# Later w_out loads, one GpSimd square instead of five, and a batch squared from PSUM, in a relu² attention and MLP kernel

## The chip, the cores and the metric

The kernel runs on one core of one Trainium2 chip. The metric is the device time of one execution in microseconds (us). Each kernel is built, checked against the reference and run several times; the number quoted is the median. All runs quoted here are in the fast state. A ratio is the mean time of one kernel's fast runs over that of the other's fast runs of the same rounds, so it is not quite the ratio of the medians quoted beside it.

## The reference, cut to what matters

```python
# q, k, v: (8, 12, 448, 64)
scores = np.matmul(q, k.transpose(0, 1, 3, 2)) / np.sqrt(64)
attn   = np.maximum(scores, 0.0) ** 2 / 448
x      = np.matmul(attn, v)            # -> 3584 tokens x 768
h      = x @ w_in                      # 768 x 2048
g      = np.maximum(h, 0.0) ** 2
out    = g @ w_out                     # 2048 x 768
```

There is no softmax: a score tile needs relu, a square and a scale on its way from PSUM to SBUF. Input and output are float32; the kernel computes in float16.

## The kernel before

A batch has three units of four heads. A unit has seven score tiles, numbered t = 0 to 6; a "round" makes one score tile, and round r is unit r // 7, tile r % 7. The opening stage (rounds 0 to 22) makes batch 0 while the weights stream in. After it TensorE works through a fixed mix of later score tiles (`sp`), attention times v (`avt`), x times w_in (`hps`) and g times w_out (`ops`). Program order on TensorE is fixed.

A score tile can be squared in two ways:

```python
def relu2(ps, dst, scale):                       # "from PSUM"
    nc.scalar.activation(out=dst, in_=ps, func=AF.Square, scale=scale)
    nc.vector.scalar_tensor_tensor(              # reads PSUM and one SBUF tile
        out=dst, in0=ps, scalar=0.0, in1=dst, op0=ALU.is_gt, op1=ALU.mult)

def relu2_wide(ps, dst, scale, eng):             # "through SBUF"
    r = rel_p.tile([P, 2, S], FP32, name="rel", tag="wide")
    nc.scalar.activation(out=r, in_=ps, func=AF.Relu, scale=scale)
    eng.tensor_mul(dst, r, r)                    # both inputs are SBUF

def soft(n, t, sp):
    at = at_p.tile([P, 2, S], FP16, name="at", tag="at")
    if n < NPE and t % 2 == 1:                   # NPE = 6, NU = 3
        relu2_wide(sp[:, :, 0:S], at, SK, nc.gpsimd if n and t == 3 else nc.vector)
    else:
        relu2(sp[:, :, 0:S], at, SK)
    ats[n, t] = at
```

So in units 0 to 5 the odd tiles go through SBUF, and tile 3 of units 1 to 5 is squared on GpSimd. GpSimd also casts q and k and issues every load that casts on the way (v, w_in, w_out). In the opening stage its order follows this table:

```python
beside = {                                       # round: what is issued beside it
    ...                                          # cut: w_in parts, transposes, casts
    8: [(turn_pe, 2, "q", act), (load_v, 1, 0)],
    9: [(cast_qk, 3, "k", pool), (cast_qk, 3, "q", pool), ...],
    10: [(load_v, 1, 1)],
    12: [(load_v, 1, 2), (load_w2, 0)],
    13: [(load_w2, 1)],
    ...
    17: [(load_w2, 2)],
    18: [(load_w2, 3)],
    16: [(cast_qk, 4, "k", pool), (cast_qk, 4, "q", pool), ...],
}
for r in range(STREAM):                          # 23 rounds, cut
    sp = scores(n, t)
    soft(n, t, sp)
    for z in late.get(r, (r - LAG,) if LAG <= r else ()):   # LAG = 3
        av(*divmod(z, TJ))
    for fn, *a in beside.get(r, ()):
        fn(*a)
```

Of the kernel before, what the change touches and what calls it, by code (L numbers as in the profile page):

```python
# [16 lines left out]
def kernel(  # L17
# [9 lines left out]
    nc = tc.nc  # L27

    B, H, S, D = q.shape
# [8 lines left out]
    NU = 3  # L38
# [5 lines left out]
    SK = 256.0  # L44
# [29 lines left out]
    def load_qk(n, w, eng):  # L74
        b, u = divmod(n, NU)
        t = raw_p.tile([P, 2, TJ * D], FP32, name=w + "f", tag=w + "f")
        src = q if w == "q" else k
        eng.dma_start(  # L78
            out=t,
            in_=src[b, 4 * u:4 * u + 4].rearrange(  # L80
                "(f e) (p t) d -> (e p) f (t d)", e=2, t=TJ))
        raw[n, w] = t

    def cast_qk(n, w, op):
        src = raw.pop((n, w))
        t = blk_p.tile([P, TJ, 2 * D], FP16, name=w + "s", tag=w + "s")
        op(t.rearrange("p t (f d) -> p f t d", f=2),  # L87
           src.rearrange("p f (t d) -> p f t d", d=D))
        blk[n, w] = t
# [7 lines left out]
    def turn_pe(n, w, op):  # L97
        src = blk.pop((n, w))
        ps = mm_p.tile([P, TJ * P], FP16, name="tps", tag="mm")
        for t in range(TJ):  # L100
            nc.tensor.transpose(ps[:, t * P:(t + 1) * P], src[:, t, :], ident)  # L101
        t = qkt_p.tile([P, TJ, P], FP16, name=w + "T", tag=w + "T")
        op(t.rearrange("p t c -> p (t c)"), ps)
        qkt[n, w] = t

    def load_v(b, us):

        if b not in vst:
            vst[b] = v_p.tile([P, NU, 2, TJ * D], FP16, name="vs", tag="vs")
        src = v[b].rearrange("(u x) (p t) d -> p u x (t d)", x=4, t=TJ)  # L110
        for r in range(2):
            rows = slice(64 * r, 64 * r + 64)
            hs = slice(1, 3) if r else slice(0, 4, 3)
            if isinstance(us, int):
                nc.gpsimd.dma_start(out=vst[b][rows, us], in_=src[:, us, hs])
            else:
                for i, h in enumerate(range(4)[hs]):
                    nc.gpsimd.dma_start(out=vst[b][rows, :, i], in_=src[:, :, h])
# [4 lines left out]
    def load_w1(i):  # L123
        nc.gpsimd.dma_start(
            out=w1[i],
            in_=moe_w_in[:, 512 * i:512 * (i + 1)].rearrange("(m p) f -> p m f", p=P))
# [26 lines left out]
    def relu2(ps, dst, scale):  # L153
        nc.scalar.activation(out=dst, in_=ps, func=AF.Square, scale=scale)  # L154
        nc.vector.scalar_tensor_tensor(  # L155
            out=dst, in0=ps, scalar=0.0, in1=dst, op0=ALU.is_gt, op1=ALU.mult)

    def relu2_wide(ps, dst, scale, eng):

        r = rel_p.tile([P, 2, S], FP32, name="rel", tag="wide")  # L160
        nc.scalar.activation(out=r, in_=ps, func=AF.Relu, scale=scale)
        eng.tensor_mul(dst, r, r)  # L162
# [82 lines left out]
    def scores(n, t):  # L245
        qT, kT = qkt[n, "q"], qkt[n, "k"]
        sp = s_p.tile([P, 2, 512], FP32, name="sp", tag="s")
        for e in range(2):
            for f in range(2):
                c = f ^ e  # L250
                r = slice(64 * f, 64 * f + 64)
                nc.tensor.matmul(  # L252
                    sp[64 * c:64 * c + 64, e, 0:S].rearrange("p (t c) -> p t c", t=TJ),
                    lhsT=kT[r, t, 64 * e:64 * e + 64],
                    rhs=qT[r, :, 64 * e:64 * e + 64], start=True, stop=True)
        return sp

    def soft(n, t, sp):
        at = at_p.tile([P, 2, S], FP16, name="at", tag="at")
        if n < NPE and t % 2 == 1:  # L260
            relu2_wide(sp[:, :, 0:S], at, SK, nc.gpsimd if n and t == 3 else nc.vector)
        else:
            relu2(sp[:, :, 0:S], at, SK)
        ats[n, t] = at
# [3 lines left out]
    def av(n, t):  # L268

        b, u = divmod(n, NU)  # L270
        if n == NU * b and t == 0:
            xts[b] = x_p.tile([P, NM, S], FP16, name="xt", tag="xt")
        vs = vst[b]
        if t == 0:
            avs_open[n] = [mm_p.tile([P, 512], FP32, name="avt", tag="mm") for _ in range(2)]
        ap = avs_open[n]
        at = ats.pop((n, t))
        for e in range(2):
            for c in range(2):
                f = c ^ e  # L280
                r = slice(64 * c, 64 * c + 64)
                nc.tensor.matmul(  # L282
                    ap[f][64 * e:64 * e + 64, 0:S],
                    lhsT=vs[r, u, e ^ c, t * D:(t + 1) * D],
                    rhs=at[r, e, :],
                    start=(t == 0), stop=(t == TJ - 1), skip_group_check=True)
        if t < TJ - 1:
            return
        for f in range(2):
            nc.scalar.activation(  # L290
                out=xts[b][:, 2 * u + f, :], in_=ap[f][:, 0:S], func=AF.Copy, scale=CX)

    pool, dve, act = nc.gpsimd.tensor_copy, nc.vector.tensor_copy, nc.scalar.copy
# [3 lines left out]
    NPE = 6  # L297
# [32 lines left out]
    with tc.manual_schedule():  # L330
        load_qk(0, "k", nc.sync)
        load_qk(0, "q", nc.scalar)
        for n in (1, 2):
            load_qk(n, "k", nc.sync)
            load_qk(n, "q", nc.sync)
        idle = const_p.tile([P, 512], FP16, name="idle", tag="idle")
        nc.vector.memset(idle, 0.0)
        ident = const_p.tile([P, P], FP16, name="ident", tag="ident")
        make_identity(nc, ident)
        for u in range(NU):  # L340
            load_v(0, u)

        warm = mm_p.tile([P, 512], FP32, name="warm", tag="mm")
        for _ in range(12):
            nc.tensor.matmul(warm, lhsT=idle[:, 0:P], rhs=idle, start=True, stop=True)
        cast_qk(0, "k", dve)
        cast_qk(0, "q", act)
        turn_pe(0, "k", dve)
        turn_pe(0, "q", dve)
        for w in "kq":  # L350
            cast_qk(1, w, pool)
        load_w1(0)

        beside = {
            1: [(load_w1, 1)],
            2: [(cast_qk, 2, "k", pool), (cast_qk, 2, "q", pool),
                (load_qk, 3, "k", nc.sync), (load_qk, 3, "q", nc.sync)],
            3: [(turn_pe, 1, "k", dve), (load_w1, 2)],
            5: [(turn_pe, 1, "q", act), (load_w1, 3)],
            7: [(turn_pe, 2, "k", dve)],  # L360
            8: [(turn_pe, 2, "q", act), (load_v, 1, 0)],
            9: [(cast_qk, 3, "k", pool), (cast_qk, 3, "q", pool),
                (load_qk, 4, "k", nc.sync), (load_qk, 4, "q", nc.sync)],
            10: [(load_v, 1, 1)],
            12: [(load_v, 1, 2), (load_w2, 0)],
            13: [(load_w2, 1)],
            14: [(turn_pe, 3, "k", dve)],
            15: [(turn_pe, 3, "q", act)],
            17: [(load_w2, 2)],
            18: [(load_w2, 3)],  # L370
            16: [(cast_qk, 4, "k", pool), (cast_qk, 4, "q", pool),
                 (load_qk, 5, "k", nc.sync), (load_qk, 5, "q", nc.sync)],
        }
        late = {21: (18, 19), 22: (20,)}
        for r in range(STREAM):
            n, t = divmod(r, TJ)
            sp = scores(n, t)
            soft(n, t, sp)
            for z in late.get(r, (r - LAG,) if LAG <= r else ()):
# [3 lines that stand above are left out]
# [3 lines left out]
    for i in range(STREAM // 2, NB):  # L386
        g = []
        for r in range(max(STREAM, 2 * i), 2 * i + 2):
            n, t = divmod(r, TJ)
            g.append((n, t, scores(n, t)))  # L390
        if i in avs:
            for t in range(TJ):
                av(avs[i], t)
        for a in g:
            soft(*a)
        if i in pushes:
            push_dense(pushes[i])
        upkeep(i)
        nxt = min([j for j in pushes if j > i] or [NB + 2])
        run_some(max(0.0, (queued - KEEP) / (nxt - i)))  # L400
# [37 lines left out]
```

## Time and profile before

The time before was 423.14 us (423.02 to 423.86, 3 runs).

| part of the execution | what TensorE does | read in |
|---|---|---|
| 0 to 34 us | opening stage, partly busy | 40-slice row |
| 34.0 to 45.0 us | idle | timeline |
| 52.75 us (sixth slice) to the end | busy 9 tenths or more, but for the last slice (5) | 40-slice row |

The page: the span, TensorE's busy time (us, share, instructions), TensorE's busy tenths in 40 slices of 10.55 us, and the clock granted to TensorE in tenths of full speed.

```profile
span 422.0 us, 7567 instructions
PE 394.7 (94%) x3104; PEld 200.4 (47%) x3104; DVE 248.9 (59%) x300; ACT 260.0 (62%) x407; POOL 80.9 (19%) x101
PE   6771699999999999999999999999999999999995
PEclk9866599999999999999999999999999999999999
```

The fourth slice is a hole in a kernel that is otherwise full. The list of waits for 30 to 50 us (who waited for whom: us in total, times, longest) names the cause and what stood before it:

```profile
PE avt L282 <- POOL at L162: 11.0, 1, 11.0
POOL vs L115 <- DMA w_1_91<-in_moe_w_in_dram: 5.7, 1, 5.7
POOL w_0_94 L129 <- DMA w_2_92<-in_moe_w_in_dram: 4.8, 1, 4.8
POOL w_1_95 L129 <- DMA w_3_93<-in_moe_w_in_dram: 3.1, 1, 3.1
```

TensorE waits once, for 11 us, for a square on GpSimd (line 162 is the multiply of `relu2_wide`). GpSimd's timeline (start, duration, instruction, in brackets the idle time before it and its releaser) shows the queue in front of that square:

```profile
31.53 0.60 POOL L115 DMA_DIRECT2D vs<-in_v_dram  x1 [5.71 <-DMA w_1_91<-in_moe_w_in_dram]
36.90 0.78 POOL L129 DMA_DIRECT2D w_0_94<-in_moe_w_out_dram  x1 [4.77 <-DMA w_2_92<-in_moe_w_in_dram]
40.76 0.74 POOL L129 DMA_DIRECT2D w_1_95<-in_moe_w_out_dram  x1 [3.09 <-DMA w_3_93<-in_moe_w_in_dram]
41.50 0.94 POOL L87 CAST ks<-kf 128x896 f16<-128x896 f32 x1
42.38 0.94 POOL L87 CAST qs<-qf 128x896 f16<-128x896 f32 x1
43.28 1.68 POOL L162 TENSOR_TENSOR at<-rel 128x896 f16<-128x896 f32 x1
```

ScalarE had the square's input ready at 31.95 us (its relu ran from 31.00 for 0.95). The square itself is short, but three DMA issues ahead of it were each held until an earlier DMA had landed. TensorE's timeline shows the hole and what follows:

```profile
33.65 0.38 PE L252 MATMUL sp<-qT,kT 64*64 64x448 f16 x4 [1.08 <-ACT rel L161]
45.01 0.59 PE L282 MATMUL avt<-at,vs 64*64 64x448 f16 x4 [10.97 <-POOL at L162]
48.64 5.09 PE L176 MATMUL hps<-xt,w_0_90 128*128 128x448 f16 x15
```

The first w_in matmul (`hps`) starts at 48.64. It marks the start of the dense stage.

### The profile page before, as it was taken

To read this page: it belongs to the slowest core of one execution; us is meant where nothing else is said; L and a number is where in the kernel's file an instruction comes from. 1 tells how busy PE (TensorE), PEld (TensorE's weight loads), DVE (VectorE), ACT (ScalarE), POOL (GpSimd) and SP (SyncE) were. 2 spreads that over 40 slices of the span, in tenths; PEclk is the share of its full clock that TensorE was granted. 3 is DMA by queue.
4 is the path that set the end of the run, shared out by engine and by line. 5 is a ranking of instruction groups with operands and counts; after the bars stand their busy time and mean duration, and the time that the engine had idled before them with its cause. 6 is when DMAs were issued, how large, how long until landed. Compare 5 with 4: busy or idle time off the path is not lost.

```text
span 422.0 us, 7567 instructions
## 1 busy us (share of the span) xinstructions
PE 394.7 (94%) x3104; PEld 200.4 (47%) x3104; DVE 248.9 (59%) x300; ACT 260.0 (62%) x407; POOL 80.9 (19%) x101
## 2 busy tenths in 40 slices
PE   6771699999999999999999999999999999999995
PEld 2330245554445444544545545545545545555563
DVE  3973378656885676756763866666755776142200
ACT  3882388767876676756765767667666677243211
POOL 6732744221312021111112111200100000000000
PEclk9866599999999999999999999999999999999999
DMA  8999996279724936293727925491713110111132
GB/s 254 295 278 211 245 206 136 45 175 230 171 84 87 204 114 168 64 200 54 190 76 139 221 94 147 87 198 32 170 39 81 39 39 1 39 37 40 37 77 75
DMA packets 62947, 53.58 MB, mean 127 GB/s; under 512 B 35776, under 2 KB 59328, under 8 KB 62912
## 3 DMA queue, kind: packets, MB, share of 16 engines
q1 hardware_dynamic: 50672, 40.84, 38.9%
q0 software_dynamic: 11968, 11.80, 17.2%
q8 instruction: 24, 0.39, 0.4%
q10 hardware_dynamic: 272, 0.46, 0.3%
q14 instruction: 11, 0.09, 0.1%
HBM read 45.61 MB, written 11.01 MB: 134 GB/s over the span
## 4 chain that ended last, share of the span: by engine, by line
PE 88%; DMA 8%; POOL 1%; issue 1%; SPq 1%; ACT 0%; DVE 0%; POOLq 0%
PE hps L176 36%; PE ops L204 36%; PE sp L252 9%; PE avt L282 7%; DMA w_2_92<-in_moe_w_in_dram 5%; DMA qf<-in_q_dram 3%; SPq L78 1%; POOL qs L87 0%; PE tps L101 0%; POOL at L162 0%; DVE at L155 0%; ACT at L154 0%; POOL w_0_94 L129 0%; POOL ks L87 0%; ACT osb L211 0%
## 5 line engine op out<-in xcount | busy, mean ns | idle before, releaser
L155 DVE SCALAR_TENSOR_TENSOR at<-sp,at 128x896 f16<-128x896 f32 x150 | 157.4, 1087 | 92.7 <-ACT at L154 92.3
L154 ACT ACTIVATE at<-sp 128x896 f16<-128x896 f32 x150 | 130.4, 915 | 77.1 <-PE sp L252 76.4
L204 PEld LDWEIGHTS <-g 128*128 128x128 f16 x896 | 84.4, 98 | 67.8 <-issue 13.7
L155 DVE SCALAR_TENSOR_TENSOR g<-hps,g 128x448 f16<-128x448 f32 x128 | 75.8, 619 | 44.0 <-ACT g L154 43.8
L154 ACT ACTIVATE g<-hps 128x448 f16<-128x448 f32 x128 | 67.7, 551 | 29.9 <-PE hps L176 29.3
L252 PE MATMUL sp<-qT,kT 64*64 64x448 f16 x672 | 53.5, 376 | 9.9 <-DVE at L155 4.8
L282 PE MATMUL avt<-at,vs 64*64 64x448 f16 x672 | 43.4, 365 | 11.2 <-POOL at L162 11.0
L211 ACT ACTIVATE osb<-ops 128x384 f32<-128x384 f32 x56 | 27.8, 496 | 38.0 <-PE ops L204 33.0
L204 PE MATMUL ops<-w_3_97,g 128*128 128x384 f16 x224 | 47.9, 327 | 0.0
L204 PE MATMUL ops<-w_2_96,g 128*128 128x384 f16 x224 | 46.6, 327 | 0.0
L87 POOL CAST ks<-kf 128x896 f16<-128x896 f32 x23 | 22.4, 974 | 125.9 <-DMA kf<-in_k_dram 98.9
L204 PE MATMUL ops<-w_1_95,g 128*128 128x384 f16 x224 | 46.1, 326 | 0.0
L204 PE MATMUL ops<-w_0_94,g 128*128 128x384 f16 x224 | 45.9, 326 | 0.0
L176 PE MATMUL hps<-xt,w_0_90 128*128 128x448 f16 x192 | 41.1, 366 | 0.0
L176 PE MATMUL hps<-xt,w_3_93 128*128 128x448 f16 x192 | 39.2, 353 | 0.0
L176 PE MATMUL hps<-xt,w_1_91 128*128 128x448 f16 x192 | 39.0, 353 | 0.0
L176 PE MATMUL hps<-xt,w_2_92 128*128 128x448 f16 x192 | 39.0, 353 | 0.0
L252 PEld LDWEIGHTS <-kT 64*64 64x64 f16 x672 | 16.5, 107 | 41.5 <-issue 38.7
L282 PEld LDWEIGHTS <-vs 64*64 64x64 f16 x672 | 21.7, 110 | 23.6 <-issue 13.5
L176 PEld LDWEIGHTS <-w_0_90 128*128 128x128 f16 x192 | 18.7, 101 | 19.6 <-issue 5.0
L176 PEld LDWEIGHTS <-w_1_91 128*128 128x128 f16 x192 | 18.1, 98 | 18.5 <-issue 2.7
L176 PEld LDWEIGHTS <-w_2_92 128*128 128x128 f16 x192 | 18.1, 98 | 18.5 <-issue 2.7
(35 smaller groups left out, 164.6 us busy)
## 6 DMA issues: line engine op xcount, KB each, us to landing
kf<-in_k_dram SPq DMA_DIRECT2D x24, 448.0 KB, 4.8
out_dram<-osb SPq DMA_DIRECT2D x56, 192.0 KB, 2.7
qf<-in_q_dram SPq DMA_DIRECT2D x23, 448.0 KB, 5.7
vs<-in_v_dram POOLq DMA_DIRECT2D x24, 168.0 KB, 5.5
vs<-in_v_dram POOLq DMA_DIRECT2D x12, 112.0 KB, 10.9
w_0_90<-in_moe_w_in_dram POOLq DMA_DIRECT2D x1, 768.0 KB, 13.5
w_1_91<-in_moe_w_in_dram POOLq DMA_DIRECT2D x1, 768.0 KB, 20.3
w_2_92<-in_moe_w_in_dram POOLq DMA_DIRECT2D x1, 768.0 KB, 21.8
```

The lines of the kernel that those rows point to most:

```text
L78: eng.dma_start(out=t, in_=src[b, 4 * u:4 * u + 4].rearrange("(f e) (p t) d -> (e p) f (t d)", e=2, t=TJ))
L87: op(t.rearrange("p t (f d) -> p f t d", f=2), src.rearrange("p f (t d) -> p f t d", d=D))
L154: nc.scalar.activation(out=dst, in_=ps, func=AF.Square, scale=scale)
L155: nc.vector.scalar_tensor_tensor(out=dst, in0=ps, scalar=0.0, in1=dst, op0=ALU.is_gt, op1=ALU.mult)
L176: nc.tensor.matmul(cell[0][:, 0:S], lhsT=w1[f // 4][:, m, (f % 4) * P:(f % 4 + 1) * P], rhs=xt[:, m, :], start=(m == 0), stop=(m == NM - 1))
L204: nc.tensor.matmul(cell[0][:, 0:HALF], lhsT=gt[f][:, tb * P:(tb + 1) * P], rhs=w2[f // 4][:, f % 4, hf * HALF:(hf + 1) * HALF], start=(f = ...
L211: nc.scalar.activation(out=cell[1][:, hf * HALF:(hf + 1) * HALF], in_=cell[0][:, 0:HALF], func=AF.Copy, scale=CO)
L252: nc.tensor.matmul(sp[64 * c:64 * c + 64, e, 0:S].rearrange("p (t c) -> p t c", t=TJ), lhsT=kT[r, t, 64 * e:64 * e + 64], rhs=qT[r, :, 64 ...
L282: nc.tensor.matmul(ap[f][64 * e:64 * e + 64, 0:S], lhsT=vs[r, u, e ^ c, t * D:(t + 1) * D], rhs=at[r, e, :], start=(t == 0), stop=(t == TJ ...
```

## The change

Its intent: keep squares that TensorE needs soon out of GpSimd's queue, issue w_out behind the casts of unit 4, load v of batch 1 in four DMAs instead of six, and take batch 1's odd tiles from PSUM.

```diff
     def soft(n, t, sp):
         at = at_p.tile([P, 2, S], FP16, name="at", tag="at")
-        if n < NPE and t % 2 == 1:
-            relu2_wide(sp[:, :, 0:S], at, SK, nc.gpsimd if n and t == 3 else nc.vector)
+        if n < NU and t % 2 == 1:
+            relu2_wide(sp[:, :, 0:S], at, SK, nc.gpsimd if n == 1 and t == 3 else nc.vector)
...
-            8: [(turn_pe, 2, "q", act), (load_v, 1, 0)],
+            8: [(turn_pe, 2, "q", act), (load_v, 1, slice(None))],
...
-            10: [(load_v, 1, 1)],
-            12: [(load_v, 1, 2), (load_w2, 0)],
-            13: [(load_w2, 1)],
...
-            17: [(load_w2, 2)],
-            18: [(load_w2, 3)],
             16: [(cast_qk, 4, "k", pool), (cast_qk, 4, "q", pool),
                  (load_qk, 5, "k", nc.sync), (load_qk, 5, "q", nc.sync)],
+            17: [(load_w2, 0), (load_w2, 1)],
+            19: [(load_w2, 2), (load_w2, 3)],
```

There are thus three separable parts: the square of unit 2 tile 3 (from GpSimd to VectorE), the DMA order, and batch 1 (units 3 to 5) from PSUM.

## The prediction

> **What bounds the kernel now.** TensorE is 94% busy; from 49 us to the end the slice row shows it at 9 tenths or more, and the chain of waits is matmuls there: no gap to win. The opening stage (batch 0, to 49 us) differs: in the list of waits TensorE's `avt` matmuls wait 10.97 us for GpSimd's square (idle from 34.0 to 45.0 us in the timeline). ScalarE (11.0 us) and VectorE (10.8 us) idle with it. The chain of waits runs through this hole: the DMA of w_in part 2 until 36.6, GpSimd's issues and casts, the square from 43.3 to 45.0.
>
> **Why the square is late.** Its input (`rel`, unit 2 tile 3) was ready at about 31.9 us. Ahead of it in GpSimd's order stand the last piece of v (batch 1), held 5.7 us until w_in part 1 landed, w_out part 0, held 4.8 us until part 2 landed, w_out part 1, held 3.1 us until part 3 landed (40.7), and two casts of unit 4 (1.8 us). Counted by issue, each held DMA waits for the eighth GpSimd DMA before it. It is a queue-order stall, not a lack of GpSimd throughput (19% busy).
>
> **What the change does.**
> - Unit 2 tile 3 goes to VectorE, where a square takes 1.08 us (GpSimd 1.68). TensorE no longer depends on GpSimd behind held DMAs here.
> - v of batch 1 takes 4 DMAs instead of 6, so w_out parts wait for w_in DMAs two places earlier. The casts of unit 4 come before them, at about 24 to 27 us, not 41.5.
> - Batch 1's odd tiles become VectorE multiplies from PSUM (1.09 us against 1.08 for a square); ScalarE is unchanged (0.92 against 0.91). VectorE gets four ops of 1.1 us more, and PSUM score tiles come free after VectorE, not after ScalarE.
>
> **Critical path.** Replaying VectorE from 31.9 us: tile 17 ends at 33.0, tiles 18 to 21 at about 34.0, 35.1, 36.1, 37.2. So the first w_in matmul starts at 37.7 to 38.5 instead of 48.64: 10.1 to 10.9 us saved. TensorE's order is unchanged and it is full after that, so the shift should reach the end.
>
> Clock: the stretch table shows the granted clock at 0.50 from 36 to 52.5 us, and the first 15 w_in matmuls took 5.03 us against 2.95 later. [...] Without the gap the clock may be full when the dense stage starts: 0 to 2 us more, I count 1.
>
> Costs: w_out is needed 11 us earlier, from about 65 us (now 75.7), all of it by 67. Now it lands by 61.5; I expect 56 to 61, so no wait, but the DMA engines are backlogged until 66 us. Later release of PSUM in batch 1, where the transposes' copies also sit: 0 to 1 us, I count 0.5.
>
> **Prediction.** 423.1 - 10.5 - 1 + 0.5 = 412.1 us, range 410.2 to 414.4. Faster by over 2% 0.89, within 2% 0.10, slower 0.01.
>
> **Right if** the gap at 34 us is gone, the first w_in matmul starts near 38, the dense stage keeps its length, w_out issues between 26 and 42 us, and VectorE has four ops more. **Wrong if** w_out or w_in is now waited for (gap before `ops` at about 65 us), casts of unit 5 behind the last w_out delay transposes near 58 us, score matmuls wait on VectorE in batch 1, or the opening stage turns out DMA-paced so that TensorE waits elsewhere.

The sum comes to 423.1 - 10.5 - 1 + 0.5 = 412.1 us. The 1 us for the clock stands as my estimate, from 5.03 us against 2.95 for 15 w_in matmuls.

## The result, and the profile after

The changed kernel took 413.08 us (412.86 to 413.27, 4 runs) against 423.42 us for the kernel before in the same rounds; the ratio is 0.9755, 95% interval 0.9738 to 0.9772. That is 10.3 us less. The page, with the same rows as before:

```profile
span 411.3 us, 7560 instructions
PE 394.0 (96%) x3104; PEld 199.7 (49%) x3104; DVE 252.8 (61%) x304; ACT 259.7 (63%) x407; POOL 74.0 (18%) x95
PE   6847999999999999999999999999999999999995
PEclk9695999999999999999999999999999999999999
```

TensorE's busy time is the same (394.7 and 394.0 us); only the hole is gone. Its timeline over the same rounds:

```profile
33.62 0.59 PE L252 MATMUL sp<-qT,kT 64*64 64x448 f16 x4 [0.85 <-ACT rel L161]
34.69 1.01 PE L282 MATMUL avt<-at,vs 64*64 64x448 f16 x8
36.34 0.59 PE L252 MATMUL sp<-qT,kT 64*64 64x448 f16 x4 [0.65 <-DVE at L155]
37.86 5.24 PE L176 MATMUL hps<-xt,w 128*128 128x448 f16 x15
```

The first `hps` moved from 48.64 to 37.86, 10.78 us earlier. From that mark to the end it is 422.0 - 48.64 = 373.4 us before and 411.3 - 37.86 = 373.4 us after. So the whole gain is made in the opening stage and nothing is given back later. GpSimd still waits for DMAs, as its timeline shows, but no TensorE work stands behind them:

```profile
26.96 0.83 POOL L129 DMA_DIRECT2D w<-in_moe_w_out_dram  x1
31.61 0.74 POOL L129 DMA_DIRECT2D w<-in_moe_w_out_dram  x1 [3.83 <-DMA w<-in_moe_w_in_dram]
39.33 0.74 POOL L129 DMA_DIRECT2D w<-in_moe_w_out_dram  x1 [6.97 <-DMA w<-in_moe_w_in_dram]
43.47 0.74 POOL L129 DMA_DIRECT2D w<-in_moe_w_out_dram  x1 [3.40 <-DMA w<-in_moe_w_in_dram]
```

The table of stretches (stretch, its length, TensorE's busy time, granted clock, DMA share, GB/s) shows that the clock did not come up earlier relative to the work:

```profile
30.00:32.00 2.00, 0.59 (x12) 1.00 1.15 279
32.00:34.00 2.00, 1.15 (x15) 0.54 1.15 276
34.00:36.00 2.00, 1.70 (x20) 0.50 1.17 283
40.00:42.00 2.00, 2.00 (x7) 0.50 1.24 204
42.00:44.00 2.00, 2.00 (x22) 0.90 1.26 202
```

Even without the 11 us hole the clock halved, at 32.2 us (a mean of 0.54 from 32 to 34 is full clock for less than 0.2 us), and the first 15 `hps` took 5.24 us (5.09 before).

### The profile page after: what moved, and what is told of

The parts are those of the page before. It is cut to its first block, busy times and chain, and to the rows that moved or that the text cites. A ratio compares the mean times of both kernels' runs of the same rounds, so it can differ in the third digit from the quotient of the medians.

```text
span 411.3 us, 7560 instructions
## 1 busy us (share of the span) xinstructions
PE 394.0 (96%) x3104; PEld 199.7 (49%) x3104; DVE 252.8 (61%) x304; ACT 259.7 (63%) x407; POOL 74.0 (18%) x95
## 4 chain that ended last, share of the span: by engine, by line
PE 91%; ACT 4%; DVE 2%; DMA 1%; issue 1%
PE hps L176 37%; PE ops L204 36%; PE sp L252 10%; PE avt L282 7%; ACT at L154 2%; ACT rel L161 1%; DMA kf<-in_k_dram 1%; DVE at L155 1%; PE tps L101 1%; ACT qT L103 0%; ACT xt L290 0%; DVE at L162 0%; DVE ks L87 0%; DVE kT L103 0%; DVE qT L103 0%
## 5 line engine op out<-in xcount | busy, mean ns | idle before, releaser
L155 DVE SCALAR_TENSOR_TENSOR at<-sp,at 128x896 f16<-128x896 f32 x159 | 166.3, 1085 | 82.1 <-ACT at L154 81.7
L154 ACT ACTIVATE at<-sp 128x896 f16<-128x896 f32 x159 | 137.7, 915 | 70.4 <-PE sp L252 70.4
L176 PE MATMUL hps<-xt,w 128*128 128x448 f16 x768 | 157.5, 356 | 0.0
L204 PE MATMUL ops<-w,g 128*128 128x384 f16 x896 | 156.8, 326 | 0.0
L176 PEld LDWEIGHTS <-w 128*128 128x128 f16 x768 | 73.1, 99 | 75.1 <-issue 13.5
L154 ACT ACTIVATE g<-hps 128x448 f16<-128x448 f32 x128 | 67.7, 551 | 29.7 <-PE hps L176 29.1
L118 POOL DMA_DIRECT2D vs<-in_v_dram x28 | 17.4, 629 | 49.1 <-PE avt L282 48.3
L290 ACT ACTIVATE xt<-avt 128x448 f16<-128x448 f32 x48 | 23.6, 553 | 2.6 <-PE avt L282 2.5
L87 POOL CAST qs<-qf 128x896 f16<-128x896 f32 x23 | 23.2, 1009 | 6.7 <-DMA qf<-in_q_dram 6.7
L162 DVE TENSOR_TENSOR at<-rel 128x896 f16<-128x896 f32 x8 | 10.1, 1258 | 0.7 <-ACT rel L161 0.6
L161 ACT ACTIVATE rel<-sp 128x896 f32<-128x896 f32 x9 | 8.3, 922 | 2.2 <-PE sp L252 2.2
```

Source lines behind the costliest of these rows:

```text
L87: op(t.rearrange("p t (f d) -> p f t d", f=2), src.rearrange("p f (t d) -> p f t d", d=D))
L118: nc.gpsimd.dma_start(out=vst[b][rows, :, i], in_=src[:, :, h])
L155: nc.vector.scalar_tensor_tensor(out=dst, in0=ps, scalar=0.0, in1=dst, op0=ALU.is_gt, op1=ALU.mult)
L176: nc.tensor.matmul(cell[0][:, 0:S], lhsT=w1[f // 4][:, m, (f % 4) * P:(f % 4 + 1) * P], rhs=xt[:, m, :], start=(m == 0), stop=(m == NM - 1))
L204: nc.tensor.matmul(cell[0][:, 0:HALF], lhsT=gt[f][:, tb * P:(tb + 1) * P], rhs=w2[f // 4][:, f % 4, hf * HALF:(hf + 1) * HALF], start=(f = ...
L290: nc.scalar.activation(out=xts[b][:, 2 * u + f, :], in_=ap[f][:, 0:S], func=AF.Copy, scale=CX)
```

## The experiments

Twelve kernels ran, in three groups; each group shared one chip. The kernel before had medians of 424.12, 423.88 and 423.69 us in them.

Theory A was mine: the gain is only that TensorE stops waiting for a square queued behind held DMA issues. Rivals were B (the DMA order itself, as the stage is DMA-paced) and C (GpSimd is too slow for the square).

### e1: only the square of unit 2 tile 3

```diff
-... nc.gpsimd if n and t == 3 else nc.vector)
+... nc.gpsimd if n and n != 2 and t == 3 else nc.vector)
```

> The kernel before, with only unit 2 tile 3 squared on VectorE; DMA order and batch 1 as before. Theory A (the gain is only that TensorE stops waiting for a square queued behind held DMA issues on GpSimd): the 11 us gap goes, first w_in matmul near 38 us, time about 413 us (412.5 to 414); at most 0.5 us is lost because GpSimd's casts of unit 4 still come at 41.5 to 43.3 us, just before the transposes that need them (43.5 us in the changed kernel). Theory B (the opening stage is DMA-paced and the reorder of the w_out and v loads is what counts): stays near 423.

Measured: 415.59 us (414.62 to 416.97), ratio 0.9803 (0.9772 to 0.9834). The hole at 34 us was gone and the first `hps` started at 37.69, so B falls. The time is still 1.6 us above the forecast range. TensorE waited 0.55 and 0.31 us for the casts of unit 4, as expected. But 2.15 us of waiting that no theory had foreseen came at 50.6 to 52.7 us, in front of a score matmul. VectorE's timeline has the reason: the square of a batch-1 tile, which takes 1.08 us elsewhere, took three times that.

```profile
48.22 3.44 DVE L162 TENSOR_TENSOR at<-rel 128x896 f16<-128x896 f32 x1 [0.18 <-ACT rel L161]
```

### e2: only the DMA edits

The edit is the second half of the diff of the change (`beside`), with `soft` as before.

> The kernel before, with only the DMA edits (v of batch 1 in 4 DMAs, w_out behind the casts of unit 4); unit 2 tile 3 stays on GpSimd, where its square now stands ahead of the w_out DMAs. Theory A (queue order): the square runs at about 32 to 33.6 us, the gap goes as well, time about 413 us (412.5 to 414), so each half of the change alone takes the whole gain and they do not add. Theory C (GpSimd is too slow for the square, moving it to VectorE is what counts): most of the gap stays, 420 or more.

Measured: 418.33 us (418.12 to 419.54), ratio 0.9876 (0.9858 to 0.9895). GpSimd's square of unit 2 tile 3 ran from 33.08 to 34.76 us, and TensorE did not wait for it; the 11 us hole was gone:

```profile
33.08 1.68 POOL L162 TENSOR_TENSOR at<-rel 128x896 f16<-128x896 f32 x1 [5.61 <-ACT rel L161]
```

So C falls as well: GpSimd is quick enough when it is free. My number was missed by over 4 us, again by a later gap: 3.38 us in front of a score matmul at 54.70, while a VectorE square took 5.04 us from 48.61.

### e3 and e4: the two DMA edits apart

```diff
 e3, v of batch 1 in four DMAs; w_out stays at rounds 12, 13, 17, 18
-            8: [(turn_pe, 2, "q", act), (load_v, 1, 0)],
-            10: [(load_v, 1, 1)],
-            12: [(load_v, 1, 2), (load_w2, 0)],
+            8: [(turn_pe, 2, "q", act), (load_v, 1, slice(None))],
+            12: [(load_w2, 0)],
 e4, w_out at rounds 17 and 19; v of batch 1 stays in six DMAs
-            12: [(load_v, 1, 2), (load_w2, 0)],
-            13: [(load_w2, 1)],
-            17: [(load_w2, 2)],
-            18: [(load_w2, 3)],
+            12: [(load_v, 1, 2)],
+            17: [(load_w2, 0), (load_w2, 1)],
+            19: [(load_w2, 2), (load_w2, 3)],
```

> The kernel before, with only v of batch 1 in 4 DMAs instead of 6. If each held GpSimd DMA waits for the eighth before it, the second w_out part now waits for w_in part 1 (lands at about 31.3 us) instead of part 3 (40.7): square from about 34.0 to 35.7 us, first w_in matmul near 40.5, time about 416 us (415 to 417). If the hold is a full DMA queue or bandwidth and not the count, the square stays at 43 us and the time near 423.

> The kernel before, with only the w_out DMAs moved behind the casts of unit 4; v of batch 1 stays in 6 DMAs. The last piece of v is then the only held DMA ahead of the square, released when w_in part 1 lands (about 31.4 us): casts 32.1 to 33.9, square to 35.6 us, first w_in matmul near 40.5, time about 416 us (415 to 417). If the wait were for w_out's bandwidth and not for the order, it should be as the full change, 413.

Measured: e3 416.99 us (416.36 to 418.29), ratio 0.9843; e4 418.30 us (416.78 to 419.03), ratio 0.9865. Both tested what I had counted in the trace of the kernel before: that each of its three held GpSimd DMAs was released when the eighth GpSimd DMA before it had landed (issued at 31.53, 36.90 and 40.76 us, where w_in parts 1 to 3 had landed at about 31.3, 36.6 and 40.5). GpSimd's timeline of e3:

```profile
31.48 0.75 POOL L129 DMA_DIRECT2D w<-in_moe_w_out_dram  x1 [5.94 <-DMA w<-in_moe_w_in_dram]
34.00 1.68 POOL L162 TENSOR_TENSOR at<-rel 128x896 f16<-128x896 f32 x1
```

The second w_out part, released at 40.76 before, was released at 31.48, when w_in part 1 had landed, because it had moved two places up in the count. The square followed at 34.00, against 43.28. In e4 the last piece of v was issued at 31.74 (the profile puts that wait down to score matmuls, which had long ended; w_in part 1 was issued at 11.0 and took 20.5 us to land) and the square followed at 34.11. So in these traces the hold went by the count of DMAs; the runs do not tell whether the chip or the kernel's framework sets it. TensorE waited 0.75 us (e3) and 1.71 us (e4) for that square, and the first `hps` started at 39.36 and 39.47. The times were 1.0 and 2.3 us above the forecast of about 416, e4 outside its range, and both had the late gap: 2.38 us (e3) and 3.53 us (e4), with VectorE squares of 3.67 and 5.19 us.

### e5: only batch 1 from PSUM

```diff
-        if n < NPE and t % 2 == 1:
+        if n < NU and t % 2 == 1:
```

> The kernel before, with only batch 1's odd tiles taken from PSUM by VectorE (no GpSimd squares there); DMA order and unit 2 tile 3 as before. Theory A: off the critical path, the 11 us gap stays, time 423 to 424. Rival (GpSimd relief in batch 1 brings part of the gain): 420 or less.

Measured: 423.75 us (423.29 to 424.17), ratio 1.0006 (0.9984 to 1.0028). By itself this part does nothing.

### e6: the changed kernel without batch 1 from PSUM

```diff
 against the changed kernel
-        if n < NU and t % 2 == 1:
-            ... nc.gpsimd if n == 1 and t == 3 else nc.vector)
+        if n < NPE and t % 2 == 1:
+            ... nc.gpsimd if n and n != 2 and t == 3 else nc.vector)
```

> The changed kernel, with batch 1's odd tiles squared through SBUF as before (tile 3 on GpSimd). Theory A: within 0.5 us of the changed kernel, 412.6 to 413.6. If the later release of PSUM costs what I put down (0.5 us), it is faster by that; if GpSimd squares behind held DMAs hurt batch 1, slower.

Measured: 418.68 us (416.77 to 419.65, 6 runs), ratio 0.9880 (0.9855 to 0.9906). Theory A missed by over 5 us: the part that is worth nothing alone (e5) is worth about half of the gain once the other parts are in. TensorE's timeline and then VectorE's:

```profile
54.28 0.59 PE L252 MATMUL sp<-qT,kT 64*64 64x448 f16 x4 [4.65 <-DVE at L155]
54.80 5.53 PE L176 MATMUL hps<-xt,w 128*128 128x448 f16 x15
```

```profile
47.29 5.93 DVE L162 TENSOR_TENSOR at<-rel 128x896 f16<-128x896 f32 x1 [0.18 <-ACT rel L161]
53.15 1.08 DVE L155 SCALAR_TENSOR_TENSOR at<-sp,at 128x896 f16<-128x896 f32 x1
```

One VectorE square (unit 3 tile 5) took 5.93 us. The multiply behind it frees a PSUM score tile, so TensorE's next scores waited 4.65 us, and after that gap TensorE was slow again (15 `hps` in 5.53 us, against 3.00 and 3.01 for the two groups of 15 at 42.87 and 46.30). GpSimd's timeline in those microseconds has no pause:

```profile
47.08 0.94 POOL L87 CAST ks<-kf 128x896 f16<-128x896 f32 x1
47.97 1.69 POOL L162 TENSOR_TENSOR at<-rel 128x896 f16<-128x896 f32 x1
49.60 0.93 POOL L87 CAST qs<-qf 128x896 f16<-128x896 f32 x1
50.47 0.93 POOL L87 CAST ks<-kf 128x896 f16<-128x896 f32 x1
51.35 0.92 POOL L87 CAST qs<-qf 128x896 f16<-128x896 f32 x1
```

GpSimd's last cast ends at 52.27, and the VectorE square ends at 53.22, 0.95 us later, which is about the whole length of a free square (1.08). So it made next to no progress until GpSimd fell idle. (The text for e9 below counts two casts before the square on GpSimd; the timeline has one.)

The square `tensor_mul(dst, r, r)` has two SBUF inputs; the multiply from PSUM has one. A square of that kind on VectorE and a cast or square on GpSimd held each other up in these traces, and in both directions. In e1 the VectorE square (48.22 to 51.66, 3.44 us) waited, by its length, for a square and a cast on GpSimd, until 50.71. Then it ran (0.95 us to its end), and GpSimd's next cast was held; it took 1.81 us, where one alone takes 0.93:

```profile
50.64 1.81 POOL L87 CAST ks<-kf 128x896 f16<-128x896 f32 x1
```

The same happened in e4 (a cast of 1.79 us) and twice in the opening stage of the changed kernel (casts of 1.81 and 1.79 us beside VectorE squares of 1.64 and 1.70 us). So the VectorE squares that met a run of GpSimd work waited for one to five of its instructions (they took 1.64 to 5.93 us instead of 1.08); no run shows what decides which engine goes first.

That such a square gets nowhere while GpSimd casts and squares back to back, and that a multiply from PSUM is not held, was theory P for the last group. Its rival, theory Q, was that TensorE waits for the late GpSimd square of unit 3 tile 3.

### e9 and e10: P against Q

```diff
 e9, against e6: the blocked tile, unit 3 tile 5, from PSUM
-        if n < NPE and t % 2 == 1:
+        if n < NPE and t % 2 == 1 and (n, t) != (3, 5):
 e10, against e6: unit 3 tile 3 squared through SBUF on VectorE, not on GpSimd
-... nc.gpsimd if n and n != 2 and t == 3 else nc.vector)
+... nc.gpsimd if n in (1, 4, 5) and t == 3 else nc.vector)
```

> As e6 (418.7 us), with one tile more taken from PSUM: unit 3 tile 5, whose VectorE square took 5.93 us in e6 (47.3 to 53.2) while GpSimd ran two casts, a square and three casts without a pause to 52.3. The GpSimd order, with its square of unit 3 tile 3, is unchanged. Theory P (a VectorE multiply that reads two SBUF inputs gets no access while GpSimd works back to back; one that reads PSUM is not held): the multiply takes 1.1 us, the 4.65 us gap at 50 us goes, time 413 to 414. Theory Q (TensorE waits for the late GpSimd square): the gap stays, 418 to 419.

> As e6, with unit 3 tile 3 squared on VectorE through SBUF instead of on GpSimd; unit 3 tile 5 also through SBUF, as in e6. Theory P: GpSimd still runs four casts back to back from about 47.1 to 50.6 us, so the square of tile 5 still takes about 4 us instead of 5.93 and a gap of about 3 us stays: time 416 to 418. Theory Q: with no GpSimd square to wait for, the gap goes: 413 to 414.

Measured: e9 412.79 us (412.55 to 413.11), ratio 0.9751; e10 416.37 us (415.19 to 417.51), ratio 0.9835. The changed kernel on the same chip took 412.96 (e12 below). In e9 GpSimd worked without a pause as before, from 47.32 to 52.51, and squared unit 3 tile 3 as late as in e6:

```profile
48.22 1.69 POOL L162 TENSOR_TENSOR at<-rel 128x896 f16<-128x896 f32 x1
```

but VectorE's two multiplies from PSUM in the middle of it ran at full speed (2.09 us for two):

```profile
48.18 2.09 DVE L155 SCALAR_TENSOR_TENSOR at<-sp,at 128x896 f16<-128x896 f32 x2 [0.18 <-ACT at L154]
```

TensorE had no gap, and the time was that of the changed kernel. In e10 the GpSimd square was gone, but four casts back to back (47.64 to 51.20) held up the VectorE square through SBUF all the same (4.56 us), and TensorE waited 3.41 us:

```profile
53.20 0.49 PE L252 MATMUL sp<-qT,kT 64*64 64x448 f16 x4 [3.41 <-DVE at L155]
```

VectorE's timeline has two squares through SBUF before that gap:

```profile
43.38 1.08 DVE L162 TENSOR_TENSOR at<-rel 128x896 f16<-128x896 f32 x1
47.59 4.56 DVE L162 TENSOR_TENSOR at<-rel 128x896 f16<-128x896 f32 x1
```

P's forecast held in both (e9 came 0.2 us below its range), Q's in neither. The first of these two squares overlapped a DMA issue on GpSimd (43.97 to 44.71) and was not slowed (1.08 us); the second lay beside the four casts (4.56 us).

In the kernel before, the squares of batch 1 had missed this collision: its VectorE square at 59.38 started as GpSimd's run of casts ended (59.47). Taking the hole out moved TensorE, ScalarE and VectorE 11 us forward, but GpSimd stayed tied to the landings of w_in (last release at about 43 us), so the two came to lie on each other. So the timelines explain why the PSUM part is worth nothing before (e5) and over 5 us after (e6); no run shifted GpSimd's casts alone to test it.

### e11: the changed kernel without the DMA edits

The edit takes `soft` from the changed kernel and `beside` from the kernel before.

> The changed kernel with the DMA edits undone (v of batch 1 in 6 pieces, w_out at its old places); squares as in the change. If the DMA edits only bring the casts of unit 4 forward: TensorE waits about 0.9 us at 42 us for those casts (0.55 and 0.31 us in e1) and nothing else, time 413 to 414.5. If they are needed for more, 415 or above.

Measured: 412.66 us (412.46 to 412.94), ratio 0.9746 (0.9714 to 0.9778), beside 412.96 for the changed kernel and just below the forecast of 413 to 414.5. In the profiled execution TensorE did not even wait for the casts of unit 4 (they ended at 43.23, and the transposes ran at 43.09 and 43.49). With both changes to `soft` in place, the DMA edits bring nothing measurable.

### e7: dummy matmuls where TensorE waits

```diff
 against the changed kernel, at the end of each opening round
+            if r == 17:
+                fill = mm_p.tile([P, 512], FP32, name="fill", tag="mm")
+            for _ in range({17: 6, 19: 4, 21: 3}.get(r, 0)):
+                nc.tensor.matmul(fill, lhsT=idle[:, 0:P], rhs=idle, start=True, stop=True)
```

> The changed kernel, with 13 dummy matmuls (128x512, result not used) put on TensorE where it waits in the last rounds of the opening stage, to keep its granted clock up. In the changed kernel the clock fell to 0.50 at about 33 us and rose only at 43; the first 15 w_in matmuls took 5.24 us against 2.95 warm. If TensorE's low activity in those last rounds is the cause: clock 1.00 at 38 us, those 15 matmuls near 3.0 us, time about 411 us. If the clock falls all the same or the dummies delay the scores: 413 or more.

Measured: 411.18 us (411.05 to 412.27, 4 runs), ratio to before 0.9715 (0.9693 to 0.9738), against 0.9755 and, on a third chip, 0.9747 for the changed kernel. The granted clock was 1.00 in every 2 us stretch from 30 to 44 us (0.97 from 28 to 30, before the first dummy at 30.56). TensorE's timeline:

```profile
30.56 1.46 PE L383 MATMUL fill<-idle 128*128 128x512 f16 x6 [0.88 <-ACT xt L290]
38.00 3.01 PE L176 MATMUL hps<-xt,w 128*128 128x448 f16 x15
```

The dummies filled waits that existed anyway (the first `hps` starts at 38.00 instead of 37.86), and the first 15 `hps` took 3.01 us instead of 5.24. This version beats the kernel before. That it beats the changed kernel is not shown clear of noise. The two did not run on one chip, and by the ratios (0.9715 against 0.9755 and 0.9747) the lead is 1.4 to 1.7 us, with intervals that meet or overlap. One of its four executions, the one of 412.27 us, had a mean granted clock of 0.980, as the changed kernel has (0.973 to 0.983); the other three had 0.989 or 0.990. The 2.2 us less in the first 15 `hps` are those of one execution.

The record of the granted clock shows how busy TensorE was before the clock changed. In the traces of the kernel before and of the changed kernel its changes lie whole multiples of 3.41 us apart (1 to 108 of them), at 11.94, 15.35, 22.18, 29.01, 35.83, 52.90 and 421.54 us in the one and at 11.70, 18.52, 32.18, 42.42 and 411.06 us in the other; `prof LABEL --windows` over such a stretch of 3.41 us gives TensorE's busy time in it. In the changed kernel the clock fell at 32.18, after a stretch in which TensorE was busy for 1.59 us (0.47 of it). In e12 a stretch with 1.84 us (0.54) kept the clock and the next, with 1.70 us (0.50), ended it. In e7 the stretch from 28.13 had 2.42 us (0.71) and kept it; without its dummies it would have had about 1.43 us (0.42, an estimate from the same trace). Counted over the traces of the kernel before and the changed kernel, a full clock fell after all 7 stretches at 0.47 or less and after none of 221 at 0.54 or more; a halved one rose after 5 stretches at 0.93 or more and stayed after 8 at 0.84 or less.

### e8: how near w_out is to being late

```diff
 against the changed kernel
-            19: [(load_w2, 2), (load_w2, 3)],
     def upkeep(i):
         for n in range(NU, NUN):
+            if n == NU and i == 12:
+                load_w2(2)
+                load_w2(3)
```

> The changed kernel, with the last two w_out parts issued after the v loads of batch 2. In the changed kernel the last part lands at 63.8 us and is needed near 67.7. If the margin is those 4 us: issue near 47 to 48, landing 67 to 70, a TensorE gap of 0.5 to 3 us before the first output matmuls that use them, time 413.5 to 416. If DMAs land earlier when fewer are outstanding: no gap, 413.

Measured: 415.05 us (413.87 to 417.02), ratio 0.9806. The two parts were issued from 46.37 us and took 18.7 and 22.0 us to land. TensorE waited for the later one:

```profile
69.16 2.11 PE L204 MATMUL ops<-w,g 128*128 128x384 f16 x12 [1.65 <-DMA w<-in_moe_w_out_dram]
```

In the changed kernel the last part was issued at 43.47 and took 20.3 us, so it landed at 63.8, where it is needed near 67.7. The margin is about 4 us; this experiment used it up.

### e12: the changed kernel again

> The changed kernel once more, as the yardstick for the other three on the same chip: 412.5 to 413.7.

Measured: 412.96 us (411.56 to 413.04), ratio 0.9747 (0.9716 to 0.9777). Its profiled execution was its fastest, 411.56: there the clock was still up at 34 to 36 us (0.97) and back at 40 (1.00 from 40 to 42), and the first 15 `hps` took 3.71 us. The other three took 412.89 to 413.04. So the same kernel spends more or less time at the low clock from one execution to the next: the mean granted clock was 0.973 to 0.983 over these four and the four of the result.

## Why the prediction was right, and where its steps were not

The time was right (412.1 forecast, 413.08 measured, inside 410.2 to 414.4), and so was the mechanism of the gain at 34 us. That all of it reached the end was in part luck, as the fourth point says.

- **The stall behind held DMAs.** Right. The hole went, and e1 and e2 show that either taking the square off GpSimd or taking the held DMAs from in front of it removes it. e3 and e4 confirm the count of eight.
- **First w_in matmul at 37.7 to 38.5, 10.1 to 10.9 us saved.** Right: 37.86, or 10.78 us, and it reached the end undiminished.
- **Clock, 1 us counted.** Mis-sized, because its cause was mistaken: it measured nothing in the profiled execution (5.24 us for the first 15 `hps`, 5.09 before). I had blamed the low clock on the 11 us hole. But it fell at 32.18 us without the hole too, after a stretch of 3.41 us in which TensorE was busy for 0.47; and in the kernel before it fell at 35.83, only 1.8 us into the hole, after a stretch with 0.54 us of matmuls (0.16), not a wholly idle one. The same 15 matmuls took 3.71 or 5.24 us in two executions of the changed kernel. The clock is worth about 2 us here by the traces (5.24 us against 3.01 in e7); e12's execution with 3.71 us was 1.3 to 1.5 us faster than its other three.
- **Batch 1 from PSUM, a cost of 0.5 us.** Wrong, and the one real failure of reasoning. I costed the multiplies by their lengths in a trace where they met no contention (1.09 against 1.08 us) and left out what would newly overlap once the hole was gone. Alone the part costs nothing (e5). In the whole change e6 shows that it protects over 5 us: without it a VectorE square through SBUF runs into GpSimd's bunched casts and takes 5.93 us. e9 shows that one tile makes the difference. The total came out right because the change had this protection in it, not because the prediction saw the need: that was luck.
- **The DMA edits.** I described them as helpful, without a number. e11 shows no measurable effect; e8 shows that issuing w_out late has a price close by.
- **w_out landing from 56 to 61 us, issued from 26 to 42 us.** Missed: the last part was issued at 43.47 and landed at 63.8. No wait came of it.

The sum as measured is 10.8 for the hole and 0 for the clock; the PSUM term should have been 0 against the kernel before, with a loss of over 5 us if left out.

What stays open: no run took out one of e7's three groups of dummies, no timed comparison of e7 and the changed kernel was made on one chip, and what decides whether VectorE or GpSimd goes first when both want to run is not known (in e10 the square's recorded start, 47.59, comes before the cast's, 47.64, and the square waited).

## What to carry to other kernels

A short instruction that a busy engine needs should not stand in the queue of an engine that also issues loads: look there first when the list of waits shows one long wait for an engine that is 19% busy. Before taking out a stall, ask which instructions will newly run at the same time; a VectorE multiply of two SBUF tiles beside back-to-back GpSimd casts and a square took up to 4.9 us longer here (5.93 instead of 1.08), and reading one operand from PSUM avoided it (2.09 us for two, e9). Parts of a change can be worth nothing alone and about half of the gain together, so undo one part of the whole as well as doing one part alone.
